# Attention and expert layer on one core: the scores' keys in two halves of the array, and x turned by TensorE in every batch

## Chip, core and metric

The program runs on one core of a Trainium2 chip. The core has five engines that run their own instruction streams in order: TensorE (in the profile PE, its weight loads PEld), VectorE (DVE), ScalarE (ACT), GpSimd (POOL) and SyncE (SP, which here only issues DMAs). They meet at semaphores. The metric is the device time of one execution in microseconds (us), as the median of several runs; less is better.

## What is computed

Attention over 8 batches, 12 heads, 448 tokens and a head size of 64, with root-mean-square norms on q and k, and then a layer of 8 experts that each take the 448 best tokens.

```python
q_n, k_n = rmsnorm(q, g_q), rmsnorm(k, g_k)
scores = np.matmul(q_n, k_n.transpose(0, 1, 3, 2)) / np.sqrt(64)
scores = scores - np.max(scores, axis=-1, keepdims=True)
attn = np.exp(scores)
attn = attn / (np.sum(attn, axis=-1, keepdims=True) + 1e-09)
x = np.matmul(attn, v)                      # (8, 12, 448, 64) -> 3584 tokens of 768
logits = x @ w_gate                         # 3584 x 8: the best 448 tokens for each expert, greedily
out[mask] = np.maximum(x[mask] @ w1[e], 0.0) @ w2[e]        # for each expert e
```

## The kernel before

**Tiling.** The attention works on 24 groups of four heads (three groups a batch); in a group two pairs of heads lie side by side. A head pair has seven units of up to 128 keys: per head three blocks of 128 keys, and one unit (u = 3) with the last 64 keys of both heads. q and k are split into two float16 parts, a high and a low one, that lie above each other in the 128 rows, so a unit's scores are two accumulating passes (`k1` by `q1`, `k2` by `q2`). One score task d makes two units into a tile `psc` of PSUM (ring of 2), and ScalarE makes `e` of it with one exp.

**What TensorE does in the attention**, with its lines in the profile:
- `max_score` (L482, L485): cheaper scores for the row maxima, in the tile `pm` (ring of 1) and one of `psc`; VectorE reduces them (`max_reduce`, L496). The maxima go back as a row into `q2`: ScalarE scales them into `qm`, a DMA turns them (L436, `mt<-qm`), two more put them into `q2` (L443, `q<-mt`). The scores of the group need that row.
- `scores` (L519 for a unit of 128 keys: one matmul fills all 128 columns of the array; L514 for u = 3: two matmuls, each in 64 columns of the array, write the lower and upper 64 partitions of `psc`).
- `av` (L544): e by v, always as two matmuls in 64 columns each. They are float32, and the trace shows two matmuls for each that the program has.
- `gate` (L648 to L656): the router's logits from `xt`, which is x with its features on the partitions.

The array's form, rows by columns in use, stands in the profile's rows: 128\*128 (L519, gate), 128\*64 (L514, L544, L655), 64\*128 and 64\*64 (maxima).

**x.** VectorE divides by the sums, ScalarE makes the high part of x (`x_hi`, L582), VectorE the low one (`x_lo`, L588 and L589), per head pair, into `xb` and `xm`. `x_store` writes them to memory for the experts. `xt` is made from the same tiles: in batches 0 to 6 by four DMA transposes per batch on SP's queue (`x_dma_turn`, L597 and L599); in the last batch by TensorE, per head pair hp, as soon as its x is there (`x_turn`, L623 and L626, into `pm` or `psc`, and `x_turned`, L636 on ScalarE or L638 on VectorE, from PSUM to `xt`).

**Order.** Every task has a number, and a table written out by hand of two characters per task (`ORDER`) gives the order in which all are emitted; an engine takes its own in that order. So the order on each engine is fixed, and only semaphores decide when each starts. The router and the experts follow when the attention is done, and TensorE is the only engine that is nearly always busy there too.

Of the kernel before, what the change touches and what calls it, by code (L numbers as in the profile page):

```python
# [26 lines left out]
F32 = mybir.dt.float32  # L27
F16 = mybir.dt.float16
# [61 lines left out]
class Attention:  # L90
# [500 lines left out]
    def x_dma_turn(self, b, part):  # L591
        nc = self.nc
        if part == 0:
            self.T["xt", b] = self.w.tile([128, 42, 128], F16, name="xt", bufs=1)
        t, xb, xm = self.T["xt", b], self.T["xb", b], self.T["xm", b]
        if part < 3:
            nc.sync.dma_start_transpose(t[:, 12 * part:12 * part + 12], xb[:, part].rearrange("p i c -> p (i c)"))  # L597
        else:
            nc.sync.dma_start_transpose(t[:, 36:], xm.rearrange("p i h d -> p (i h d)"))  # L599

# [11 lines left out]
    def x_turn(self, b, hp):  # L612

        nc = self.nc
        if hp == 0:
            self.T["xt", b] = self.w.tile([128, 42, 128], F16, name="xt", bufs=1)
        t, xb, xm = self.T["xt", b], self.T["xb", b], self.T["xm", b]
        p = self.ps.tile([128, 2, 512], F32, name=("pm", "psc")[hp % 3 > 0], bufs=1 + (hp % 3 > 0))
# [8 lines left out]
        self.T["tp", hp] = p  # L627

    def x_turned(self, b, hp, mid):
        p, t = self.T["tp", hp], self.T["xt", b]  # L630
# [4 lines left out]
        if hp < 4:  # L635
# [56 lines left out]
    def gate_sum(self, b):  # L692
# [21 lines left out]
                 V=2, mx=2, pm=1, psc=2, e=9, po=2, z=2, xb=2, xt=1, lsc=2)  # L714
    GATE = 3

    def plan(self):
# [136 lines left out]
        for pair in range(2 * self.NG):  # L854
# [13 lines left out]
            if hp == 5:  # L868
# [3 lines left out]
                if b < last:  # L872
                    for i in range(4):
                        add(s + P["xst"] + P["xstep"] * i, "S", 1.75 if i < 3 else 1.3, self.x_dma_turn, b, i, after=x, opens=[("xt", b)],
                            make=("xt", b, i), uses=[("xb", b)], move=(1.3, 1.5 if i < 3 else 0.75))
                if b < last:
                    for j in range(4):
                        add(s + P["gate"] + P["gates"] * j, "T", US["gate"], self.gate, b, j,
                            after=[*(("xt", b, i) for i in range(4)), "wg"], make=("pg", b), opens=[("gate", b)] if j == 0 else (),
# [5 lines left out]
                else:  # L885
                    add(s + P["gate"] + 0.2, "D", 0.2, self.gate_copy, b, after=[("pg", b)], make=("logits", b),
                        frees=[("pg", b)])
            if b == last:
                ring = ("pm", "psc")[hp % 3 > 0]
                add(s + P["xturn"], "T", US["xturn"], self.x_turn, b, hp, after=[x[hp], x[hp - hp % 2]],  # L890
                    make=("tp", hp), opens=[("xt", b)] * (hp == 0), holds=[(ring, ("xt", hp))], uses=[("xb", b), ("xt", b)])
                for mid in range(1 + hp % 2):
                    q = "AD"[hp > 3]
                    add(s + P["xtd"] + mid, q, US[f"xtd{q}{mid}"], self.x_turned, b, hp, mid,
                        after=[("tp", hp)], make=("xt", b, hp), uses=[("xt", b)], frees=[("xt", hp)])
# [8 lines left out]
    def plan_first(self, plan, g, a, t):  # L904
# [1021 lines left out]
```

## Time and profile before

| | us |
|---|---|
| median of 3 runs | 953.76 (952.52 to 955.08) |
| the profiled execution | 957.85 |
| its span, from the first instruction to the last | 956.0 |
| TensorE busy (matmuls) | 887.7 |
| VectorE, ScalarE, GpSimd busy | 625.0, 465.4, 400.1 |

The attention takes the first 456 us of the span, the router and the experts the rest. A group of rows below gives an engine's busy time in a stretch, another the waits, others single instructions with their start in us. TensorE's matmuls overlap: of two rows of the timeline the difference of their starts is what the first one costs, not its own length.

### The profile page before, as it was taken

To read this page: it belongs to the slowest core of one execution; us is meant where nothing else is said; L and a number is where in the kernel's file an instruction comes from. 1 tells how busy PE (TensorE), PEld (TensorE's weight loads), DVE (VectorE), ACT (ScalarE), POOL (GpSimd) and SP (SyncE) were. 2 spreads that over 40 slices of the span, in tenths; PEclk is the share of its full clock that TensorE was granted. 3 is DMA by queue.
4 is the path that set the end of the run, shared out by engine and by line. 5 is a ranking of instruction groups with operands and counts; after the bars stand their busy time and mean duration, and the time that the engine had idled before them with its cause. 6 is when DMAs were issued, how large, how long until landed. Compare 5 with 4: busy or idle time off the path is not lost.

```text
span 956.0 us, 25484 instructions
## 1 busy us (share of the span) xinstructions
PE 887.7 (93%) x10674; PEld 542.4 (57%) x10676; DVE 625.0 (65%) x1468; ACT 465.4 (49%) x705; POOL 400.1 (42%) x447
## 2 busy tenths in 40 slices
PE   2878989998999998999699999899999999999996
PEld 1445556665666655668465556456565555655553
DVE  6877877886677776963788777576876757234110
ACT  4866667766778676655044433333333424243110
POOL 7697878788688886720110302011112020120001
PEclk9999999999999999999599999999999999999998
DMA  6456889979899988961374929495967649483001
GB/s 165 106 121 138 172 164 205 187 182 198 191 181 218 179 202 162 181 106 58 97 256 159 274 84 222 143 250 181 217 205 221 201 148 298 150 179 119 25 18 41
DMA packets 271787, 157.84 MB, mean 165 GB/s; under 512 B 197398, under 2 KB 258838, under 8 KB 270648
## 3 DMA queue, kind: packets, MB, share of 16 engines
q1 hardware_dynamic: 247128, 129.33, 58.0%
q0 software_dynamic: 4704, 22.10, 7.7%
q10 hardware_dynamic: 19840, 4.79, 2.4%
q8 instruction: 83, 1.36, 0.6%
q14 instruction: 32, 0.26, 0.1%
HBM read 94.49 MB, written 22.02 MB: 122 GB/s over the span
## 4 chain that ended last, share of the span: by engine, by line
issue 34%; PE 8%; POOL 5%; DVE 2%; DMA 1%; SPq 1%; ACT 0%; POOLq 0%; DVEq 0%
PE ph L1689 6%; POOL rows L1622 2%; POOL out_dram L1725 2%; PE py L1706 1%; DMA stage<-in_moe_w_dram 1%; SPq L1627 1%; PE py L1655 1%; PE rp L1264 0%; DMA rows<-xd,idx 0%; POOL spacer L1724 0%; DVE or L1239 0%; DVE cmp L1249 0%; PE rp L1335 0%; ACT xt L1642 0%; ACT w2h L1605 0%
## 5 line engine op out<-in xcount | busy, mean ns | idle before, releaser
L1689 PE MATMUL ph<-xt,w1h 128*128 128x448 f16 (+2 forms) x804 | 209.7, 344 | 0.3 <-ACT xt L1642 0.3
L544 PEld LDWEIGHTS po<-v,e 128*64 128x64 f32 x5376 | 177.2, 139 | 55.3 <-issue 45.9
L544 PE MATMUL po<-v,e 128*64 128x65 f32 x5376 | 198.4, 226 | 0.9 <-DVE xm L589 0.5
L530 ACT ACTIVATE e<-psc 128x896 f32<-128x896 f32 x168 | 152.0, 916 | 83.1 <-PE psc L519 55.0
L1725 POOL DMA_INDIRECT out_dram<-y,idx x32 | 32.6, 1018 | 292.2 <-ACT y L1708 256.8
L519 PE MATMUL psc<-q,k 128*128 128x448 f16 x576 | 137.3, 360 | 10.4 <-DMA q<-mt 6.4
L1689 PE MATMUL ph<-xt,w1l 128*128 128x448 f16 (+2 forms) x402 | 135.1, 344 | 0.0
L1706 PE MATMUL py<-w2h,hl 128*128 128x384 f16 x384 | 125.0, 326 | 0.0
L1706 PE MATMUL py<-w2h,hh 128*128 128x384 f16 x384 | 125.0, 326 | 0.0
L1706 PE MATMUL py<-w2l,hh 128*128 128x384 f16 x384 | 125.0, 326 | 0.0
L496 DVE TENSOR_REDUCE mx<-pm 128x2 f32<-128x896 f32 x96 | 103.9, 1083 | 27.7 <-PE pm L485 22.2
L1689 PEld LDWEIGHTS <-w1h 128*128 128x128 f16 x804 | 74.0, 97 | 63.8 <-issue 2.1
L1677 ACT ACTIVATE hh<-ph 128x448 f16<-128x448 f32 x64 | 34.8, 544 | 143.7 <-PE ph L1689 142.0
L1706 PEld LDWEIGHTS <-hh 128*128 128x128 f16 x768 | 73.2, 97 | 46.7
L1679 DVE SCALAR_TENSOR_TENSOR hl<-ph,hh 128x448 f16<-128x448 f32 x64 | 39.3, 618 | 73.0 <-ACT hh L1677 72.9
L496 DVE TENSOR_REDUCE mx<-psc 128x2 f32<-128x896 f32 x74 | 78.1, 1058 | 10.8 <-PE psc L485 10.0
L1622 POOL DMA_INDIRECT rows<-xd,idx x32 | 32.2, 1005 | 125.3 <-PE rp L1457 65.8
L1708 ACT ACTIVATE y<-py 128x384 f32<-128x384 f32 x48 | 23.6, 491 | 124.8 <-PE py L1706 98.6
L519 PEld LDWEIGHTS <-k 128*128 128x128 f16 x576 | 46.3, 98 | 52.1 <-issue 15.7
L1609 DVE SCALAR_TENSOR_TENSOR w2l<-stage,w2h 128x768 f16<-128x768 f32 x64 | 60.1, 951 | 14.7 <-ACT w2h L1605 14.4
L1609 DVE SCALAR_TENSOR_TENSOR w1l<-stage,w1h 128x768 f16<-128x768 f32 x64 | 59.3, 950 | 3.3 <-ACT w1h L1605 3.3
L277 DVE TENSOR_REDUCE st<-sq 128x14 f32<-128x910 f32 (+1 forms) x52 | 52.4, 1017 | 11.3 <-ACT sq L265 8.9
(282 smaller groups left out, 1399.7 us busy)
## 6 DMA issues: line engine op xcount, KB each, us to landing
stage<-in_moe_w_dram SPq DMA_DIRECT2D x64, 768.0 KB
vraw<-in_v_dram SPq DMA_DIRECT2D x24, 384.0 KB
xd<-xb SPq DMA_DIRECT2D x8, 1152.0 KB
qkraw<-in_q_dram SPq DMA_DIRECT2D x23, 384.0 KB
qkraw<-in_k_dram SPq DMA_DIRECT2D x23, 384.0 KB
xd<-xm SPq DMA_DIRECT2D x16, 96.0 KB
qkraw<-in_k_dram ACTq DMA_DIRECT2D x46, 32.0 KB
qkraw<-in_q_dram ACTq DMA_DIRECT2D x44, 32.0 KB
```

The costliest lines, as they stand in the source:

```text
L277: self.nc.vector.tensor_reduce(self.stat(g, 0, a)[:, i], self.T["sq", g, i][:, self.of(a)], axis=AX.X, op=OP.add)
L496: self.nc.vector.tensor_reduce(m, p[:, :k, :448], axis=AX.X, op=OP.max)
L519: nc.tensor.matmul(p[:, i, :448], kt[:, a, n:n + 128], qt[:, a, 448 * s:448 * s + 448], start=st, stop=not st)
L530: self.nc.scalar.activation(e, p[:, :, :448], AF.Exp, scale=scale)
L544: nc.tensor.matmul(out, self.T["e", d][:, i, q0:q0 + m], self.v1[g % 2][:, self.slot(a, u, s)], start=u == us[0], stop=u == us[-1])
L1609: self.later(0.93, lambda w=w: self.nc.vector.scalar_tensor_tensor(l[:, w], v[:, w], self.WS, h[:, w], op0=OP.mult, op1=OP.subtract), k, i)
L1622: nc.gpsimd.indirect_dma_start(out=g[:n, c, :], out_offset=None, in_=self.xd, in_offset=bass.IndirectOffsetOnAxis(ap=idx[:n, c:c + 1], axi ...
L1677: nc.scalar.activation(hh, whole, AF.Relu)
L1679: self.later(0.6, lambda: nc.vector.scalar_tensor_tensor(hl, whole, 0.0, hh, op0=OP.max, op1=OP.subtract), k, 3.5, f)
L1689: nc.tensor.matmul(p, a[:, i, c], x[:, b, o], start=j == 0, stop=j == 17)
L1706: nc.tensor.matmul(p, a[:, f, s], b[:, f, o], start=st, stop=sp)
L1725: st = nc.gpsimd.indirect_dma_start(out=self.out, out_offset=bass.IndirectOffsetOnAxis(ap=self.router.idx[k][:n, c:c + 1], axis=0), in_=y[ ...
```

## The change

`scores` makes every unit as it made u = 3: two matmuls, each with 64 keys in 64 columns of the array and the same queries, in the two halves of `psc`'s partitions. `x_dma_turn` is gone; `x_turn` and `x_turned` run in every batch, in batches 0 to 6 always with the tile `pm` and with VectorE. `xt` has two buffers instead of one. The table of the order has a number for each new task.

```diff
-                if u == 3:
-                    for s in range(2):
-                        nc.tensor.matmul(p[64 * s:64 * s + 64, i, :448],
-                                         kt[:, a, 384 + 64 * s:448 + 64 * s],
-                                         qt[:, a, 448 * s:448 * s + 448], start=st, stop=not st)
-                else:
-                    s = u // 4
-                    nc.tensor.matmul(p[:, i, :448], kt[:, a, n:n + 128],
+                for h in range(2):
+                    s = h if u == 3 else u // 4
+                    nc.tensor.matmul(p[64 * h:64 * h + 64, i, :448], kt[:, a, n + 64 * h:n + 64 * h + 64],
                                      qt[:, a, 448 * s:448 * s + 448], start=st, stop=not st)
...
-    def x_dma_turn(self, b, part):
...
-            nc.sync.dma_start_transpose(t[:, 12 * part:12 * part + 12], xb[:, part].rearrange("p i c -> p (i c)"))
...
+    def turn_ring(self, b, hp):
+        return ("pm", "psc")[hp % 3 > 0] if b == self.B - 1 else "pm"
+
+    def turned_queue(self, b, hp):
+        return "A" if b == self.B - 1 and hp < 4 else "D"
...
-        if hp < 4:
+        if self.turned_queue(b, hp) == "A":
             self.nc.scalar.activation(o, p, AF.Copy)
         else:
             self.nc.vector.tensor_copy(o, p)
...
-                 V=2, mx=2, pm=1, psc=2, e=9, po=2, z=2, xb=2, xt=1, lsc=2)
+                 V=2, mx=2, pm=1, psc=2, e=9, po=2, z=2, xb=2, xt=2, lsc=2)
...
-        "4H3XDv36HzN5DwN23u4ISC3v3ZDyDxN63wNADz3a4KH+3xD+D-3zN8E03CH-I03+4hSDSE37NB4jSF384LI1NC3yI24J4kSGE14i410ESHN7"
+        "4H3XDv36HzN5DwN23u4ISC3v3ZDyDxN63wNADz3a4KH+3xD+D-3zN8E03CH-I03+4hSFSG37NB4jSH384LI1SDSENC3yI24J4kSIE14i410E"
```

All other tasks keep their places among each other on every engine; the new ones stand between them, and SP's queue loses 28 DMA transposes. TensorE, one score unit between two stretches of `av` (`k_902` and `q_1025` are one group's keys and queries, `k_1_126` and `q_0_128` the tiles `k2` and `q2`), before:

```order
631 L544 MATMUL po<-v_1_137,e 64x65 x16
632 L519 LDWEIGHTS k_902
633 L519 MATMUL psc<-q_1025,k_902 128x448
634 L519 LDWEIGHTS k_1_126
635 L519 MATMUL psc<-q_0_128,k_1_126 128x448
```

and after (the `av` ahead is L539 now; the numbers of the buffers differ):

```order
1048 L539 MATMUL po<-v_0_136,e 64x65 x8
1049 L514 LDWEIGHTS k_959
1050 L514 MATMUL psc<-q_1097,k_959 64x448
1051 L514 LDWEIGHTS k_959
1052 L514 MATMUL psc<-q_1097,k_959 64x448
1053 L514 LDWEIGHTS k_1_126
1054 L514 MATMUL psc<-q_0_128,k_1_126 64x448
1055 L514 LDWEIGHTS k_1_126
1056 L514 MATMUL psc<-q_0_128,k_1_126 64x448
```

Each matmul of 128 output partitions has become two of 64. SP's queue around the first batch's x (`mt` is the turned row of maxima on its way to `q2`), before:

```order
55 L436 DMA_TRANSPOSE mt<-qm_131 128x1x128
56 L597 DMA_TRANSPOSE xt<-xb 128x12x128
57 L443 DMA q_1_129<-mt 1x7x128 x2
58 L386 DMA_TRANSPOSE k_1716<-ks_1510 128x14x128
59 L597 DMA_TRANSPOSE xt<-xb 128x12x128
60 L386 DMA_TRANSPOSE q_1775<-qs_1699 128x14x128
```

and after:

```order
54 L436 DMA_TRANSPOSE mt<-qm_131 128x1x128
55 L443 DMA q_1_129<-mt 1x7x128 x2
56 L386 DMA_TRANSPOSE k_1900<-ks_1655 128x14x128
57 L386 DMA_TRANSPOSE q_1967<-qs_1882 128x14x128
```

The turns of x no longer stand between the maxima's row and the transposes of k and q. TensorE behind a new turn of x, after (there is no L609 or L612 at this place before; L485 follows the scores directly):

```order
3874 L609 MATMUL pm<-ident,xb 128x128
3875 L612 LDWEIGHTS xm
3876 L612 MATMUL pm<-ident,xm 128x128
3877 L612 LDWEIGHTS xm
3878 L612 MATMUL pm<-ident,xm 128x128
3879 L485 LDWEIGHTS q_5807
3880 L485 MATMUL pm<-k_1_126,q_5807 128x448
```

The maxima behind it use the same tile `pm`, so they follow VectorE's copies out of it. VectorE in batch 6 (L1124 to L1164 are a piece of the router that the attention takes in), after:

```order
541 L1134 TENSOR_SCALAR key<-keyi 128x21
542 L1164 TENSOR_TENSOR cmp<-key,hit_80 128x672
543 L630 COPY xt<-pm 128x6x128
544 L630 COPY xt<-pm 128x2x128
545 L630 COPY xt<-pm 128x6x128
546 L496 TENSOR_REDUCE mx<-pm 128x2
```

Two turns' copies stand behind the router's piece and ahead of the next reduction.

## Rows read from the trace of the kernel before

**Rows 1.** Busy time of each engine in stretches of the attention: bounds in us, their length, then PE, PEld, DVE, ACT and POOL busy with their counts, TensorE's granted clock as a share of 2.4 GHz, the mean share of the DMA engines, GB/s. The last line sums seven stretches from 100 to 440 us.

```profile
60.00:100.00 40.00, 33.69 (x540) 21.13 (x539) 32.26 (x48) 26.27 (x42) 33.13 (x33) 0.96 0.68 134
...
150.00:200.00 50.00, 49.00 (x868) 31.77 (x868) 39.10 (x65) 36.88 (x61) 40.20 (x39) 1.00 1.00 180
200.00:250.00 50.00, 46.08 (x794) 29.40 (x793) 37.37 (x63) 32.04 (x54) 41.35 (x40) 0.97 0.96 205
...
400.00:440.00 40.00, 40.00 (x768) 27.00 (x766) 21.57 (x44) 23.31 (x38) 7.90 (x8) 1.00 0.67 130
sum 340.00, PE 323.21 PEld 211.73 DVE 251.87 ACT 230.43 POOL 250.21; mean PE 46.17 PEld 30.25 DVE 35.98 ACT 32.92 POOL 35.74
```

**Rows 2.** What TensorE waited for from 100 to 440 us: the waiting line, what ended the wait; us in total, times, longest.

```profile
PE psc L519 <- DMA q<-mt: 4.9, 5, 1.7
PE pm L485 <- DVE mx L496: 3.6, 3, 3.2
PE psc L519 <- ACT e L530: 2.6, 6, 0.7
PE psc L485 <- ACT e L530: 1.9, 2, 1.2
PE pm L485 <- DMA q<-qs: 1.3, 1, 1.3
...
PE po L648 <- DMA xt<-xb: 0.6, 1, 0.6
```

**Rows 3.** TensorE in order of time at three places: start, length, line, operation, output and inputs, array form, shape, count.

```profile
397.90 1.62 PE L544 MATMUL po<-v,e 128*64 128x65 f32 x48
399.45 0.93 PE L519 MATMUL psc<-q,k 128*128 128x448 f16 x4
400.31 0.69 PE L544 MATMUL po<-v,e 128*64 128x65 f32 x16
400.93 0.36 PE L485 MATMUL pm<-k,q 64*128 64x448 f16 x2
...
414.72 0.55 PE L519 MATMUL psc<-q,k 128*128 128x448 f16 x2
415.20 0.57 PE L514 MATMUL psc<-q,k 128*64 128x448 f16 x4
415.60 0.63 PE L544 MATMUL po<-v,e 128*64 128x65 f32 x16
416.17 0.36 PE L485 MATMUL pm<-k,q 64*128 64x448 f16 x2
...
429.66 3.49 PE L544 MATMUL po<-v,e 128*64 128x65 f32 x112
432.97 0.17 PE L655 MATMUL po<-wg,xt 128*64 128x16 f16 x1
```

**Rows 4.** TensorE in the experts, first and last of 21 rows without a gap, each two matmuls in 64 columns of the array.

```profile
943.75 0.33 PE L1715 MATMUL py<-w2h,hh 128*64 128x384 f16 x2
...
947.00 0.33 PE L1715 MATMUL py<-w2h,hl 128*64 128x384 f16 x2
```

**Rows 5.** The last batch's turns of x in order of time: TensorE (L623, L626) and the row behind it, VectorE's copies out of PSUM (L638), and the weight load (PEld) that follows the first copy.

```profile
440.21 0.50 PE L623 MATMUL pm<-ident,xb 128*128 128x128 f16 x6
440.55 0.92 PE L519 MATMUL psc<-q,k 128*128 128x448 f16 x4
...
446.57 0.50 PE L623 MATMUL pm<-ident,xb 128*128 128x128 f16 x6
...
447.01 0.50 PE L623 MATMUL psc<-ident,xb 128*128 128x128 f16 x6
...
451.55 0.50 PE L623 MATMUL psc<-ident,xb 128*128 128x128 f16 x6
452.08 0.56 DVE L638 COPY xt<-psc 128x768 f16<-128x768 f16 x1
452.69 0.10 PEld L668 LDWEIGHTS <-xt 128*128 128x128 f16 x1 [0.17 <-DVE xt L638]
...
454.07 0.76 DVE L638 COPY xt<-psc 128x256 f16<-128x256 f16 x2 [0.53 <-PE psc L626]
```

**Rows 6.** SP's DMA transposes of x: line, operation, count, shortest, median and longest ns on SP's queue, first and last start; and two rows of SP's queue in order of time.

```profile
L597 SPq DMA_TRANSPOSE xt<-xb x21: 1386/2016/3305, 111.0 to 420.2; - x21
...
L599 SPq DMA_TRANSPOSE xt<-xm x7: 1211/1317/2097, 133.0 to 421.9; - x7
...
228.12 1.87 SPq L597 DMA_TRANSPOSE xt<-xb  x1
...
231.84 1.60 SPq L443 DMA_DIRECT2D q<-mt  x2
```

**Rows 7.** VectorE's reductions of `pm` among the page's costliest groups (busy us, mean ns of one, idle before and its releaser); then, from the timeline, VectorE's first and last instruction of the router's piece, and TensorE where it ends.

```profile
L496 DVE TENSOR_REDUCE mx<-pm 128x2 f32<-128x896 f32 x96 | 103.9, 1083 | 27.7 <-PE pm L485 22.2
...
390.90 0.33 DVE L1135 TENSOR_REDUCE best<-logits 128x21 f32<-128x168 f32 x1
...
396.55 0.86 DVE L1175 TENSOR_TENSOR cmp<-key,hit 128x672 bf16<-128x672 f32 x1
...
396.39 1.10 PE L544 MATMUL po<-v,e 128*64 128x65 f32 x32
397.42 0.36 PE L485 MATMUL pm<-k,q 64*128 64x448 f16 x2
```

More of the change, by code (lines that the diff above doesn't have):

```diff
@@ L589, in x_lo @@
         tt(om[:, 1], m, om[:, 0], op=OP.subtract)
-    def x_dma_turn(self, b, part):
[L592 to L596, printed above, removed]
-            nc.sync.dma_start_transpose(t[:, 12 * part:12 * part + 12], xb[:, part].rearrange("p i c -> p (i c)"))
-        else:
-            nc.sync.dma_start_transpose(t[:, 36:], xm.rearrange("p i h d -> p (i h d)"))
     def x_store(self, b, part):
@@ L615, in x_turn @@
         if hp == 0:
-            self.T["xt", b] = self.w.tile([128, 42, 128], F16, name="xt", bufs=1)
+            self.T["xt", b] = self.w.tile([128, 42, 128], F16, name="xt", bufs=self.RINGS["xt"])
         t, xb, xm = self.T["xt", b], self.T["xb", b], self.T["xm", b]
-        p = self.ps.tile([128, 2, 512], F32, name=("pm", "psc")[hp % 3 > 0], bufs=1 + (hp % 3 > 0))
+        ring = self.turn_ring(b, hp)
+        p = self.ps.tile([128, 2, 512], F32, name=ring, bufs=self.RINGS[ring])
         p = [p[:, i].bitcast(F16).rearrange("p (n c) -> p n c", c=128) for i in range(2)]
@@ L872, in plan @@
                 if b < last:
[L873 to L876, printed above, removed]
                     for j in range(4):
                         add(s + P["gate"] + P["gates"] * j, "T", US["gate"], self.gate, b, j,
-                            after=[*(("xt", b, i) for i in range(4)), "wg"], make=("pg", b), opens=[("gate", b)] if j == 0 else (),
+                            after=[*(("xt", b, i) for i in range(6)), "wg"], make=("pg", b), opens=[("gate", b)] if j == 0 else (),
                             uses=[("xt", b), ("gate", b)], holds=[("po", ("pg", b))] if j == 0 else (), modes=[int(j == 3)] * 2)
@@ L887, in plan @@
                         frees=[("pg", b)])
-            if b == last:
[L889 to L895, printed above, removed]
+            ring, q = self.turn_ring(b, hp), self.turned_queue(b, hp)
+            add(s + P["xturn"], "T", US["xturn"], self.x_turn, b, hp, after=[x[hp], x[hp - hp % 2]],
+                make=("tp", b, hp), opens=[("xt", b)] * (hp == 0), holds=[(ring, ("xt", b, hp))], uses=[("xb", b), ("xt", b)])
+            for mid in range(1 + hp % 2):
+                add(s + P["xtd"] + mid, q, US[f"xtd{q}{mid}"], self.x_turned, b, hp, mid,
+                    after=[("tp", b, hp)], make=("xt", b, hp), uses=[("xt", b)], frees=[("xt", b, hp)])
+            if b == last:
                 add(s + P["glast"], "T", 0.25 + 0.34 * (hp % 2), self.gate_last, b, hp,
@@ new lines @@
+        "ITNYEO5h4zNc47SlIU5KEPSmNd5L4-IVNe5MSnEQ0r5j4+NaERNf5lESIW5N5kNk5m50IXETNZ5OEV5QIY51EUNb48IZNg68S+Ia5nS-4ZNh"
+        "Ib5oEW6BIc6C5P4eT0IeEXT1IdNjT2Nl5R4a694bIfSxIg4gNiSySzEY5pT55qT6NmIhEZNn4AT7No6AEa4cT3NqT8Ii5r5ST40I0J0KT9Eb"
+        "5sIj5UNsEc6DNpEd5TEeNtEf4fNvEg5tTANx5V6ENrIk5vNyTBTC0LTD6G6F5uImIlTENwTF5W4d6HEhIoIn57EiTGNz6d6IIpIqTH52TINu"
+        "53Ir5wIs54TJTKTLTMSrItStSqIuTNSoSuIv0MTOEjSsEk6e6JN+Sv6fIwEl5x55TPO06KIxO3TQTREm6i6gSwO25y56EoO46h5zEnO56LOA"
+        "6jEp5+O9Er6M6OIyEqI+595XIz6P6kO8I-O1766lEs5-J06NEt58N-J2J1TSTT6mO75Y77J35ZJ4TU6nOBTV796oO6J5SpJ6TZ7B5cTaTW6p"
@@ new lines @@
+        "Eu6QTbOC6q5aEvJ7ODTcOH7ATXOITd5dJ8TYEw5eOE6R6SJ9ExOG0N0OEz78JA6r6TEyJCJBOF5b6sE+JD7bTqTrOJE-6tJE7gF0TnOM6U7C"
+        "ToTpTsF1OLF26u7EOKTtJG7F61JF62ONOOJH7D60JI6vTuOPJJ7eTvJK7G7c6wTwF363JLOQ0PF47dOVTxF5JM7HOTTyJNTz7IF67fORF77J"
+        "OUF8JO6yT+7KOST-JPF9OWFB7h7L84OX6xFA7MJQ85OaU3U47NU5FC6VOc7jJSJR65ObU6FDU0TgOdJTJUU766867kOZ6z6W64OYU1U2U87i"
+        "JVJW6XU9UAJYUBJXUC87ThUDTi89JaUEJZTjOe88676YFE7OOj0Q0RFFJbTk7POh7QFG7l7m8AFHOkFJ8C7nOf6aTl6cFI7oJc7ROiTmJdOg"
+        "7pFK6b6+Ol0SFM6ZJe7q7rFLJg7SJfUIFNUJJhOp8ZFOOn8dUKJi8b8DUFOmUL6-Oq8aUGUHUMJj70Jk8BUNJm73JlTeOo8E7tTfUOFP7sOs"
@@ new lines @@
+        "JnFQ71Ot8fFROr7u8e8cJoUPUQURFSJp7vOvFTOy8FUSFUOu758G7TFVUTOx8IFX7wJq8gOw8H8hOzUgUhJrO+0T0U8iJs8J748K7xFWP0Jt"
+        "Ui92JuUjO-JvJw94FYJxP3FZJyUk7UFa72P28jJzFb8LP17V93FcP4FdUnUoPA8kFe8M8lP9FfJ+8m95977WP7UpJ-Fg8NP6UqK0987YUrP8"
+        "Fi8n968O7XP5K18oUvK27aUwFh8PUdK4K3UxK5UeUfUlUmFjUXUZUaK67yUyUYK70V0WUzK8997ZPB8QK9PGFk8rUsKAUW9A9XPD8s81PFUb"
+        "7z0XUtUuU+9B827+PHKBPCU-UcPI9C8pUUFlKC9D9bFm8q9cPEFn9YPLKDV0PK7-V1V29ZFoKEFpPOV39E8tFqPJ9FKFPNV4Fr9aKGFt9G9I"
+        "8uPPFsKHKI9H83PS80FuKJPM8v9dPQ8RKKV89fV9VAKMKLFvA0PVKN9gV5KOA2VBPR8SA1V6V7VC9K8TFwPTFxKP9LA3PWA48WFyPUVDKQVE"
@@ L990 @@
+        "Y0Y1HcMVReY4MWHdY5CuRgRfDIMXMYDJY6MaMZYADHYBYCXvMbXxMcYDXwDLYEMeDKRiMdRkRjMfXtRlXuRoRnXsRmXyMgXzX+YJMiMhRpMj"
+        "RrRqYKYLRsMkYMRtMlRuRvMmYRYNY7MnMoRwYSMpYTRyRxYUMqY8YVRzMrS0R+R-MsYaYbYcYWMtYFYdS1YGS3S2YHYeS5S7S6S4YOYiYjY9"
+        "YkYPYfYIYlYgYXYhYmYQYYYpYrYZYtYoYsYnYuYq"
     )
```

56 lines of the change are left out of this document (20 added, 36 removed).

## The prediction

> **What bounds the kernel now.** I read the busy times by stretch first [rows 1]. From 100 to 440 us TensorE's matmuls fill 323 of 340 us, VectorE 252, GpSimd 250 and ScalarE 230. From 400 to 440 us TensorE is busy without a break. So in the attention the time is TensorE's, made of its own work and of what it waits for. The waits came next [rows 2]: on DMAs 4.9 + 1.3 + 0.6 = 6.8 us, on VectorE's reductions 3.6, on ScalarE's exp 2.6 + 1.9 = 4.5. From 150 to 200 us the DMA engines are busy all the time and TensorE still is for 49 of 50 us: busy DMA engines cost nothing there. From 60 to 100 us TensorE is busy for 33.7 of 40 us; less work on it may be lost there. Then I read the timeline of TensorE [rows 3], because busy time hides what a change of the array's form costs: the difference of two starts shows it. The change leaves the router and the experts alone, so I look for everything in the attention.
>
> **Part 1, the scores in two halves.** Prices, from differences of starts [rows 3]. Forty-eight matmuls of av take 1.55 us and sixteen take 0.62: 0.029 for one, and 0.155 for the stretch. The 112 that are followed by L655, which has the same form 128\*64, take 3.31 = 112 x 0.029 + 0.05. So of the 0.155 some 0.105 goes with the change of form behind the stretch and 0.05 with the one ahead; av behind L514 agrees, sixteen in 0.57. Four full score matmuls take 0.86 and two 0.48: 0.19 each, and 0.10 for the change of form behind them. Two pairs of L514 take 0.40: 0.19 a pair, and 0.02 for the change ahead. So av to full scores costs 0.105, full scores to av 0.10 + 0.05 = 0.15, full scores to L514 0.10 + 0.02 = 0.12.
>
> A pair in two halves costs what one full matmul did. The experts' pairs of 384 columns start (947.00 - 943.75) / 20 = 0.1625 apart [rows 4], which is 0.1896 for 448 columns. So the work itself stays the same, and the changes of form go: in the order of before av is followed by full scores 110 times, full scores by av 70 times and by L514 48 times: 110 x 0.105 + 70 x 0.15 + 48 x 0.12 = 11.6 + 10.5 + 5.8 = 27.8 us. The order of after has 187 places between scores and av, all of one form. Where this stall goes, ScalarE's exp is late next: TensorE already waits for it at eight places [rows 2], with a shorter score task by up to 0.1 us more each. That, and the first 100 us, where TensorE waits for others anyway, may take back some of it: I put 0.4 us for both, and 2 into the range.
>
> The Trainium skill speaks against this part: in "TensorEngine Tiling (Array Packing)", section Restrictions and Gotchas, columns in tiles exclude Fast Weight Load. By that rule weight loads would come to stand ahead of the pairs, a score unit would be longer than before, and the time would be that of the third rival below. The trace has such pairs without a loss [rows 4], so I go by the trace.
>
> **Part 2, x turned on TensorE.** New are 42 turns, 21 of six matmuls and 21 of eight. Six start 0.34 us before the next work, eight 0.44 [rows 5]: 21 x 0.34 + 21 x 0.44 = 16.4 us. A turn has the form 128\*128 and mostly stands between works of the form 128\*64. By the order: 25 times av ahead (0.105), 20 times scores (0.10), 21 times av behind (0.15), 19 times scores (0.12) = 2.6 + 2.0 + 3.2 + 2.3 = 10.1, less 0.5 for those that the last batch had already: 9.6. Together 26.0 us. So part 1 gives 27.8 / 8 = 3.5 us a batch and part 2 takes 26.0 / 7 = 3.7 in the seven batches that get it: **TensorE's work stays the same to 2 us** (-27.8 + 26.0 = -1.8), and what is left lies in the last batch, where TensorE is busy without a break [rows 1].
>
> The Trainium skill gives a far higher price for a turn: "TensorE: Matmul & The Clock Gate", Part 4, has some 275 ns for one 128x128 turn in a kernel. By that the 294 turns would cost 81 us instead of 16.4. In this trace they start 56 ns apart [rows 5], so I take the trace.
>
> **Part 3, the copies out of PSUM.** A turn in `pm` is copied by VectorE: 0.56 us for six blocks, 0.76 for eight [rows 5], so 21 x 0.56 + 21 x 0.76 = 27.7 us more on VectorE, which goes from 252 to some 276 of 340 us (three of the turns lie before 100 us). It keeps idle time, but `pm` has one buffer. From the start of a turn to the next use of `pm` go 2.08 - 1.55 = 0.53 us until the copy begins, 0.56 for it and 0.05 until TensorE follows: 1.14 us; for eight blocks some 1.4. Behind 3 of the 42 turns the maxima that need `pm` follow directly (as in the third place of the order above): 0.8 us of wait each for six blocks, 1.0 for eight. Behind nine more one stretch of scores or av stands between, 0.6 to 0.9 us, which covers the copy if VectorE takes it up at once; it is busy for three quarters of the time, so I take 0.2 each. One place is worse: two turns' copies stand behind the router's piece, which holds VectorE from 390.9 to 397.4 [rows 7]; the maxima at 397.42 then have the rest of one copy, a turn and a copy ahead, some 2 us (one of the three directly followed is this one). Sum: 2 x 0.9 + 2 + 9 x 0.2 = 5.6. The copies also push other rows of VectorE back by up to 0.4 us more than the turn itself delays TensorE; where a reduction is already late (3.6 us, [rows 2]) that adds up, and I take 1 us. So **6.6 us of new waits**; with VectorE free at every copy 2.6 + 1, with a reduction of 1.08 us [rows 7] ahead of it at all twelve places 2.6 + 2 + 13.
>
> **Part 4, DMAs taken away.** SP loses 21 issues of 2.0 us and 7 of 1.3 [rows 6], 51 us of a queue that runs in order, and the DMA engines lose the traffic. What stands behind these issues is the row of maxima on its way to `q2`: at 231.84 its DMAs start behind a turn of x at 228.12 [rows 6]. The waits that this can end are the 6.8 us on DMAs and the slower clock behind them (0.97 of 2.4 GHz in the stretch 200 to 250 us [rows 1], so 3% of 50 us, 1.5 us; before it stand waits on `q<-mt`): 8.3 at most, and nothing at least, since fewer transfers make none later. Not every such wait has a turn of x ahead. I take **5.5 us**.
>
> **Sum.** -1.8 + 0.4 + 6.6 - 5.5 = -0.3 us. The profiled execution is 957.85 us, its span 956.0 with 1.85 around it, and 4.1 above the median 953.76; the sum says 957.5 for such an execution and, moved to the median, 953.5. I forecast **953.5**, no change that can be told: a difference under 0.3% (2.9 us) is about what a measurement of this kernel can tell from none.
>
> **Rivals.**
> - The DMAs' relief arrives in full and `pm` doesn't bind: -1.8 - 8.3 + 2.6 = -7.5, so 946. For it: a turn can begin only when `pm`'s last reduction is over, so VectorE is often free for its copy, and the DMA engines were full. Against it: the exp and the reductions, on which TensorE waits for as long, get nothing.
> - Slower by the ring: VectorE takes up a copy one reduction late. It decides from the point at which a copy comes while a reduction runs and the next maxima stand within 1.1 us behind the turn, which is so at twelve places: 12 x 1.08 + 2.6 + 2 = 17.6 instead of 6.6, so +11 against the forecast, 964.5. Against it: VectorE is idle for a quarter of the time, and the reduction that it may be in is one of `psc` or of squares, since that of `pm` is over.
> - The pairs lose their weight loads' cover. Priced by the 0.02 that a first pair pays, on 576 former full matmuls: +11.5, so 965. Against it [rows 4]. It is what the skill's page on tiling would lead to.
> - Turns that don't overlap with what follows: 0.50 us each instead of 0.34 [rows 5], 42 x 0.16 = +6.7, so 960. The skill's 275 ns is this case at its worst (+64 us, by that page).
>
> **Chances.** Forecast 0.50 (own range 950 to 957: 0.38 within 0.3%, 0.09 faster, 0.03 slower), relief 0.26, ring 0.15, pairs 0.05, turns 0.04. So faster 0.09 + 0.26 = 0.35, same 0.38, slower 0.27. The range of 8 in 10 reaches to 945 for the relief with 1.5 us around it, and to 962, which takes in the milder half of the ring and leaves its upper half and the pairs out.
>
> **What would show it.** Score stretches between av should take 0.76 us for two units (0.86 before), and sixteen matmuls of av between scores 0.47 (0.62): if not, part 1 is wrong. Six turns should take 0.34 to the next start and show no wait of their own. Waits of TensorE on `q<-mt` and `q<-qs` should fall from 6.2 us to under 2, and new ones on VectorE's `xt` copies should come to 4 to 8 us, with one of some 2 us where the router's piece ends. The forecast is wrong if TensorE's waits as a whole, some 15 us in [rows 2], move by more than 3 us.

## The result and the profile after

The kernel after takes 961.13 us (median of 20 runs, 954.16 to 966.07), the kernel before beside it 954.3 (20 runs, 946.46 to 964.74): a ratio of 1.0076, 95% interval 1.0052 to 1.0100. It is slower by 7.2 us by the ratio (6.8 by the medians), where no change was forecast (953.5). Medians are of all runs; ratios leave out the executions that fell into a slower state of the chip, so the two can differ by some us. The profiled execution has a span of 959.4 us, against 956.0.

Busy times by stretch, the columns as in [rows 1]; the last line again sums 100 to 440 us:

```profile
60.00:100.00 40.00, 34.59 (x610) 24.20 (x609) 32.99 (x52) 25.85 (x43) 33.42 (x33) 0.96 0.63 137
...
200.00:250.00 50.00, 47.24 (x953) 34.64 (x950) 40.95 (x75) 33.63 (x57) 42.78 (x41) 1.00 0.75 186
...
400.00:440.00 40.00, 39.92 (x829) 30.78 (x831) 25.29 (x49) 22.17 (x36) 8.20 (x8) 0.96 0.38 101
sum 340.00, PE 322.45 PEld 239.82 DVE 274.74 ACT 229.06 POOL 249.85; mean PE 46.06 PEld 34.26 DVE 39.25 ACT 32.72 POOL 35.69
```

VectorE's 23 us more are the copies, and the DMA engines are no longer full (0.96 to 0.75 from 200 to 250 us). TensorE is as busy as before. What it waited for from 100 to 440 us, the answer to [rows 2]:

```profile
PE psc L514 <- ACT e L525: 4.2, 6, 1.2
PE pm L485 <- DVE mx L496: 3.7, 4, 2.5
PE pm L609 <- DVE mx L496: 2.2, 2, 1.8
PE pm L609 <- DVE xt L630: 1.0, 1, 1.0
PE psc L485 <- DVE mx L496: 1.0, 2, 0.6
...
PE pm L482 <- DVE xt L630: 0.9, 2, 0.7
...
PE pm L485 <- DVE xt L630: 0.7, 1, 0.7
...
PE psc L514 <- DMA q<-mt: 0.4, 1, 0.4
```

The waits on DMAs are gone but for 0.4 us (6.8 before), and as much wait on VectorE has come in their place: 11.2 us in all against 4.7, of which 2.6 are on the copies `xt` and most of the rest on reductions. TensorE in order of time, the answer to [rows 3, 5]:

```profile
161.89 0.51 PE L609 MATMUL pm<-ident,xb 128*128 128x128 f16 x6
162.33 0.69 PE L539 MATMUL po<-v,e 128*64 128x65 f32 x16
...
393.79 0.92 PE L514 MATMUL psc<-q,k 128*64 128x448 f16 x8
394.55 1.57 PE L539 MATMUL po<-v,e 128*64 128x65 f32 x48
395.95 0.92 PE L514 MATMUL psc<-q,k 128*64 128x448 f16 x8
...
406.65 0.64 PE L539 MATMUL po<-v,e 128*64 128x65 f32 x16
407.12 0.93 PE L514 MATMUL psc<-q,k 128*64 128x448 f16 x8
```

By the starts, two units of scores take 0.76 us, sixteen matmuls of av 0.47, forty-eight 1.40, and six turns with the change of form behind them 0.44: each price is the one forecast. The last view is the router's piece, VectorE's last row of it and what TensorE does there, the answer to [rows 7]:

```profile
396.71 1.10 PE L539 MATMUL po<-v,e 128*64 128x65 f32 x32
...
397.17 0.86 DVE L1164 TENSOR_TENSOR cmp<-key,hit 128x672 bf16<-128x672 f32 x1
398.04 0.76 DVE L630 COPY xt<-pm 128x768 f16<-128x768 f16 x2
...
398.85 0.49 PE L609 MATMUL pm<-ident,xb 128*128 128x128 f16 x6 [1.04 <-DVE xt L630]
...
400.08 0.36 PE L485 MATMUL pm<-k,q 64*128 64x448 f16 x2 [0.74 <-DVE xt L630]
...
400.60 2.87 PE L539 MATMUL po<-v,e 128*64 128x65 f32 x48
403.25 1.25 PE L514 MATMUL psc<-q,k 128*64 128x448 f16 x8
```

The two waits of 1.04 and 0.74 us are the 2 us that were forecast there. But the 48 matmuls of av behind them take 2.65 us instead of 1.40: the granted clock is 0.50 of 2.4 GHz there, 1.2 GHz (columns as in [rows 1]).

```profile
402.00:403.60 1.60, 1.60 (x30) 1.44 (x28) 0.68 (x2) 0.00 (x0) 0.00 (x0) 0.50 0.02 6
```

From the first av matmul to the last the attention takes 412.74 us before and 415.36 after, TensorE busy and the rest (columns as in [rows 1]). Before, and after:

```profile
38.08:450.82 412.74, 386.78 (x6864) 253.46 (x6865) 302.50 (x501) 279.67 (x455) 301.61 (x289) 0.98 0.84 168
```

```profile
38.56:453.92 415.36, 388.69 (x7725) 288.36 (x7725) 326.36 (x564) 278.87 (x455) 301.18 (x289) 0.98 0.66 144
```

TensorE is idle for 26.0 us before and 26.7 after. This line, and idle = length less busy, is the measure for what follows. It differs between executions of one kernel: a second one of before, and two of after in which the experts were changed (further down), have

```profile
38.24:449.55 411.31, 385.55 (x6864) 252.66 (x6865) 300.43 (x501) 278.64 (x455) 301.52 (x289) 0.99 0.82 168
```

```profile
38.95:449.35 410.40, 385.46 (x7724) 285.89 (x7725) 325.77 (x564) 278.88 (x455) 301.49 (x289) 0.99 0.66 146
```

```profile
39.55:449.15 409.60, 385.50 (x7725) 285.82 (x7725) 326.23 (x564) 278.71 (x455) 301.29 (x289) 0.99 0.66 146
```

### The profile page after: what moved, and what is told of

The parts are those of the page before. It is cut to its first block, busy times and chain, and to the rows that moved or that the text cites. A ratio compares the mean times of both kernels' runs of the same rounds, so it can differ in the third digit from the quotient of the medians.

```text
span 959.4 us, 27248 instructions
## 1 busy us (share of the span) xinstructions
PE 888.0 (93%) x11546; PEld 576.8 (60%) x11546; DVE 649.0 (68%) x1531; ACT 464.3 (48%) x705; POOL 399.1 (42%) x447
## 4 chain that ended last, share of the span: by engine, by line
issue 34%; PE 10%; POOL 5%; DVE 2%; POOLq 0%; DVEq 0%
PE ph L1678 6%; POOL rows L1611 2%; PE py L1695 2%; POOL out_dram L1714 2%; PE py L1704 0%; PE rp L1253 0%; POOL spacer L1713 0%; DVE or L1228 0%; PE rp L1324 0%; DVE cmp L1238 0%; DVE w1l L1598 0%; DVE xt L1633 0%; PE py L1626 0%; POOLq L1910 0%; DVE or L1480 0%
## 5 line engine op out<-in xcount | busy, mean ns | idle before, releaser
L539 PEld LDWEIGHTS po<-v,e 128*64 128x64 f32 x5376 | 184.8, 140 | 37.6 <-issue 21.0
L539 PE MATMUL po<-v,e 128*64 128x65 f32 x5376 | 198.3, 226 | 1.2 <-DVE xm L584 0.8
L514 PE MATMUL psc<-q,k 128*64 128x448 f16 x1344 | 157.2, 359 | 6.2 <-ACT e L525 4.5
L514 PEld LDWEIGHTS <-k 128*64 128x64 f16 x1344 | 72.4, 111 | 42.1 <-issue 13.6
L1611 POOL DMA_INDIRECT rows<-xd,idx x32 | 32.1, 1004 | 124.0 <-PE rp L1446 65.2
L1594 ACT ACTIVATE w1h<-stage 128x1536 f16<-128x1536 f32 x32 | 47.3, 1477 | 22.1 <-DMA stage<-in_moe_w_dram 22.0
```

The costliest lines, as they stand in the source:

```text
L514: nc.tensor.matmul(p[64 * h:64 * h + 64, i, :448], kt[:, a, n + 64 * h:n + 64 * h + 64], qt[:, a, 448 * s:448 * s + 448], start=st, stop=n ...
L539: nc.tensor.matmul(out, self.T["e", d][:, i, q0:q0 + m], self.v1[g % 2][:, self.slot(a, u, s)], start=u == us[0], stop=u == us[-1])
L1594: self.nc.scalar.activation(h, v, AF.Copy, scale=self.WS)
L1611: nc.gpsimd.indirect_dma_start(out=g[:n, c, :], out_offset=None, in_=self.xd, in_offset=bass.IndirectOffsetOnAxis(ap=idx[:n, c:c + 1], axi ...
```

## The experiments

All ratios are to the kernel before, runs of the same chip; 0.001 is 0.95 us. Theory A says that the prices of the four parts were right and one place, the router's piece, went wrong. Theory B says that TensorE's time was counted wrongly: work that is taken from it comes back as waits. Where an expectation names a theory A or B and says what it means, it is one of its own.

### The scores alone

```diff
 # the kernel before, with the new scores()
+                for h in range(2):
+                    nc.tensor.matmul(p[64 * h:64 * h + 64, i, :448], kt[:, a, n + 64 * h:n + 64 * h + 64], ...
```

Expected: 

> The kernel before with the scores in two halves; x is turned by DMA as before. By the prediction's prices the changes of form go, 27.8 us, less what ScalarE's exp, the maxima's row and the full DMA queue take back once TensorE is faster: a ratio of 0.971 if nothing takes any back, 0.980 to 0.985 if a third to a half is lost to them. If halves cost TensorE something that the two traces do not show, the ratio is 0.995 or more.

Measured: 945.65 us, 0.9927 (0.9901 to 0.9953). The attention and its waits:

```profile
38.27:443.19 404.92, 367.60 (x7431) 273.64 (x7431) 299.51 (x501) 278.36 (x455) 301.07 (x289) 0.97 0.85 171
```

```profile
PE psc L514 <- DMA q<-mt: 8.6, 5, 4.4
PE psc L514 <- ACT e L525: 6.5, 8, 2.9
PE pm L485 <- DVE mx L496: 3.7, 3, 3.2
PE pm L485 <- DMA q<-qs: 2.6, 2, 1.5
```

TensorE is busy 19.2 us less and idle 11.4 more (37.3). Three quarters of the 27.4 us that part 1 gives are not in the time, more than the third to a half that was expected. This fits theory B.

### The turns alone

```diff
 # the kernel after, with the old scores()
+                    nc.tensor.matmul(p[:, i, :448], kt[:, a, n:n + 128], ...
```

Expected: 

> The kernel after with full scores of 128 keys, as before; the turns of x stay on TensorE. By the prediction's prices the scores' changes of form come back, some 27 us less about 5 for turns that then stand beside work of their own form: 22 us above the kernel after, 29 above the kernel before, a ratio of 1.031 to the latter. If ScalarE, VectorE or the maxima's row sets the pace in the kernel after, a slower TensorE hides some of it: 1.015 to 1.025.

Measured: 962.47 us, 1.0098 (1.0068 to 1.0129), less than either expectation.

```profile
38.13:458.43 420.30, 402.75 (x7159) 270.53 (x7159) 324.44 (x564) 280.15 (x455) 301.34 (x289) 0.99 0.67 142
```

TensorE is busy 16.0 us more than before and idle 8.4 less (17.6). By the ratios (1.0098 and 1.0076, whose intervals overlap) the halves bring the kernel after only 2 us in the company of the turns, though its TensorE is busy 14.1 us less: 9.1 of them are idle time again in these two traces. But this run's attention is longer than all three of the kernel after, by 5 to 11 us (420.30 against 415.36, 410.40 and 409.60), and its experts are 4.7 us shorter (458.2 from their first matmul to their last, against 462.9). So the ratio of whole runs hides part of what the halves do in the attention.

### The router's piece moved

```diff
 # the kernel after; the table of the order, batch 6 (hp 1 and 2 are the pairs behind the router's piece)
-early, x_turn(6,1), ..., x_turned(6,1,0), x_turned(6,1,1), x_turn(6,2), x_turned(6,2,0), max_scores(156), ..., max_reduce(156)
+x_turn(6,1), x_turned(6,1,0), x_turned(6,1,1), early, ..., max_scores(156), ..., max_reduce(156), x_turn(6,2), x_turned(6,2,0)
```

Expected: 

> The kernel after, with the router's piece on VectorE moved behind the first turn's copies, and the second turn with its copy moved behind the next maxima of the same ring. Theory A, that the time was lost at this one place (1.0 + 0.7 us of waits at 398 to 400 us, and 3.4 us at half the clock behind them, worth 1.6): 3.0 to 3.5 us less than the kernel after, a ratio of 1.0035 to 1.0045 to the kernel before. Theory B, that the new turns cost time at many places and this is only the one that this execution shows: at most 1 us less, 1.006 to 1.008.

Measured: 959.97 us, 1.0067 (1.0037 to 1.0098). That lies where this expectation's theory B has it, but the interval takes in theory A too. Its attention took 410.90 us, 4.5 less than in the first trace of the kernel after but not less than in the other two, and its experts 3.2 us more than in the first: 466.1 against 462.9. The experts come below.

### The DMA turns left out

```diff
 # the kernel before
+        if b == 0 and part == 0:
+            self.fixed = self.w.tile([128, 48, 128], F16, name="xt", bufs=1)
+        self.T["xt", b] = self.fixed[:, b:b + 42]
+        if b > 0:
+            return
...
```

Expected: 

> The kernel before without the DMA turns of x in batches 1 to 6: the router's logits of these batches are made from shifted views of the first batch's turned x, so the choice of tokens is another one, with the same amount of work everywhere. This is the DMAs' relief alone, without the turns on TensorE. The prediction took 5.5 us (6/7 of it here, 4.7: a ratio of 0.995); in full it would be 8.3 (7.1 here, 0.9925). Theory A, that the waits on DMAs in the profiled execution, which was 3.5 us above the median, were more than the usual ones: 1 to 2.5 us, 0.9975 to 0.999. If no wait of the usual execution has such a transfer ahead: 1.000.

Measured: 948.12 us, 0.9945 (0.9914 to 0.9977): 5.2 us, where the prediction has 4.7 for these six batches. Its price for the DMAs' relief agrees; the interval, 2.2 to 8.2 us, takes in the full relief (7.1) as well, and little of the doubt in the expectation (1 to 2.5).

```profile
38.12:445.20 407.08, 386.12 (x6864) 253.20 (x6865) 300.86 (x501) 279.10 (x455) 301.63 (x289) 0.98 0.70 150
```

### Both gains without a price

The last edit together with the new `scores`.

Expected: 

> The kernel before with the scores in two halves and without the DMA turns of x in batches 1 to 6: the router's logits of these batches are made from shifted views of the first batch's turned x, so the choice of tokens is another one, with the same amount of work. It is the two gains without any turn on TensorE or copy. With the halves alone TensorE's work fell by 22 us and the time by 7, and its waits on the maxima's row (10.9 us) and on q (2.6) were DMA waits. If the DMAs keep the halves' gain back, both go with the turns: 928 to 933 us, a ratio of 0.974 to 0.979. If the two gains only add up, 0.9927 and 0.9945: 0.987. If ScalarE and VectorE pace TensorE by now: 0.990 or more.

Measured: 933.07 us, 0.9769 (0.9728 to 0.9809): 22 us. The halves alone bring 7, the DMA turns left out 5, both together 22. In the attention alone, against the mean of four traces of before (411.64 us, all four are listed below), it is 6.7, 4.6 and 19.5. So the DMA turns kept the halves' gain back: the waits on the row of maxima, `q<-mt`, fall from 8.6 us to 1.8, while those on `q<-qs` stay (2.6 and 2.7).

```profile
38.52:430.64 392.12, 364.68 (x7430) 272.39 (x7431) 300.28 (x501) 277.82 (x455) 301.17 (x289) 0.98 0.73 156
```

```profile
PE psc L514 <- ACT e L525: 7.6, 11, 2.3
PE pm L485 <- DVE mx L496: 3.6, 3, 3.2
PE pm L485 <- DMA q<-qs: 2.7, 1, 2.7
PE psc L514 <- DMA q<-mt: 1.8, 2, 1.4
```

Against the run before this one TensorE is busy 21.4 us less, not 27.8, and idle 6.5 more. Most of that is on DMAs once again: from the first av matmul to the last the waits on them go from 1.3 us to 6.6, and those on ScalarE's exp from 8.9 to 11.1.

### The copies: left out, and on ScalarE

```diff
 # the kernel after; first run of the two
+        if 0 < b < self.B - 1:
+            return        # in x_turned; xt of these batches is a view of the first batch's
 # second run
-        return "A" if b == self.B - 1 and hp < 4 else "D"
+        return "A" if b < self.B - 1 or hp < 4 else "D"
```

Expected without them: 

> The kernel after without the copies of turned x out of PSUM in batches 1 to 6; TensorE still makes the turns, and the router's logits of these batches come from shifted views of the first batch's turned x, so the choice of tokens is another one. VectorE has 23.8 us less to do, and the ring of the maxima is free as soon as a turn is over. If the copies are what keeps the halves' gain back in the kernel after, 6 to 10 us less than it: a ratio to the kernel before of 0.997 to 1.001. If only the waits on the copies go, 2.6 us, and at the router's piece 3.3: 1.001 to 1.004. If ScalarE's exp and the maxima's reductions are late without them too: 1.005 to 1.008.

Expected on ScalarE: 

> The kernel after with all copies of turned x out of PSUM on ScalarE instead of VectorE. If VectorE's load is what holds the kernel after up (7 us of TensorE's waits there are on reductions, 3 on the copies themselves), it is 3 to 6 us faster than the kernel after: a ratio to the kernel before of 1.001 to 1.005. If ScalarE's exp is as late as VectorE's reductions (TensorE waits 7 us for it in the kernel after), the waits only move: 1.006 to 1.014.

Measured: without the copies 952.12 us, 0.9968 (0.9942 to 0.9995); on ScalarE 971.47, 1.0165 (1.0114 to 1.0216). So by whole runs the 36 turns' copies cost the kernel after 9 us by the medians, 10 by the ratios. On ScalarE the time is above both expectations; it is the worse place, and the same ring then waits for it.

```profile
PE pm L609 <- ACT xt L628: 5.8, 7, 2.0
PE pm L485 <- ACT xt L628: 4.6, 6, 1.2
PE pm L482 <- ACT xt L628: 3.8, 5, 1.3
```

The attention without the copies, in the slowest of its twelve executions (957.07 us):

```profile
38.85:449.02 410.17, 385.27 (x7724) 285.72 (x7725) 306.02 (x511) 278.93 (x455) 301.90 (x289) 0.99 0.67 146
```

With the copies it was 415.36, 410.40 and 409.60 us. So the traces show between 5 us and nothing for the copies in the attention, and the 9 to 10 us of the whole runs are not found there. These runs don't separate the ring from VectorE's load either.

### The kernel before again

Expected: 

> The kernel before once more, for a second execution with a profile: the ratio is 1.000. If the waits on DMAs of the first profile (6.8 us from 100 to 440 us) are usual, this profile shows 5 to 8 us of them again; if they were much by chance, under 4.

Measured: 954.02 us, 0.9974 (0.9944 to 1.0005). Its profile has 5.8 us of waits on `q<-mt` and 2.6 on `q<-qs`: usual waits, not chance (8.4 us together, just above the 5 to 8 expected). Its attention took 411.31 us.

### One expert alone

```diff
-        for k in range(8):
+        for k in range(1):        # in the experts; the lists for k = 1 to 7 are left out too
```

Expected before: 

> The kernel before with the first expert alone: the attention and the router's first choice are whole, the other seven experts are left out. In the experts TensorE waits up to 6 us for VectorE around 550 to 605 us in some executions, whatever the change; here that part is gone, and the time is that of the attention. From the profiled executions: attention to 450.5, router 33.5, first expert some 60 to 80 us, end 9.

Expected after: 

> The kernel after with the first expert alone, the other seven left out. If the whole of the 7 us of the medians lies in the attention: 6 to 8 us above the kernel before with one expert. If the profiled executions tell the usual attention, 453.9 against 450.8 and 449.6: 3 to 4.5 us above, and the rest is the experts'.

Expected with the router's piece moved: 

> The kernel after with the router's piece moved (as in the third experiment) and the first expert alone, the other seven left out. Theory A, that the one place at the router's piece costs the kernel after 3.3 us (1.8 of waits and 1.6 of half clock): 2.8 to 4 us below the kernel after with one expert. Theory B, that this place is only where one execution shows what is lost elsewhere in another: less than 1 us below.

Measured: 545.26 (ratio 0.5708, 0.5681 to 0.5735), 547.85 (0.5741, 0.5714 to 0.5767) and 545.54 us (0.5718, 0.5692 to 0.5744). So the attention and the first expert account for 2.6 us of the 7 by the medians, 3.2 by the ratios, below what was expected for either case; the move of the router's piece gives back 2.3 of them, between its two theories. The intervals are wider than these differences. In the profile of the second run the router's place has the same two waits as in the kernel after (for the second the profile names a DMA that ended last):

```profile
395.84 0.49 PE L609 MATMUL pm<-ident,xb 128*128 128x128 f16 x6 [1.05 <-DVE xt L630]
397.07 0.37 PE L485 MATMUL pm<-k,q 64*128 64x448 f16 x2 [0.74 <-DMA vraw<-in_v_dram]
...
397.56 1.62 PE L539 MATMUL po<-v,e 128*64 128x65 f32 x48
399.01 0.93 PE L514 MATMUL psc<-q,k 128*64 128x448 f16 x8
```

The 48 matmuls of av take 1.45 us: the clock did not fall this time. In the third run neither wait is there.

### The experts' waits taken away

One place where the experts differ between executions is a pair of DMA transposes of the third expert's tokens. SP's queue in the kernel before and with the scores alone, and the wait of TensorE behind the first:

```profile
583.79 11.19 SPq L1627 DMA_TRANSPOSE xt<-rows  x2
...
603.92 0.17 PE L1349 MATMUL rp<-cs,sums 128*128 128x8 f16 x1 [2.65 <-DVE cs L1345]
```

```profile
575.33 6.13 SPq L1622 DMA_TRANSPOSE xt<-rows  x2
```

The pair holds the queue for some 6 us or some 12, and behind it stands a load of weights, ScalarE's and VectorE's split of them, and the router's step on which TensorE waits. With 6 us the experts take 457.6 us (scores alone), with 12 they take 462.5 (before), 462.9 (after) and 466.1 (router's piece moved). The seven other traces that have all experts and these transposes go the same way: 457.6 to 458.2 us where the pair takes 5.7 to 5.9 (turns alone, both gains, SP's queue in another order), 462.1 to 464.1 where it takes 11.3 to 12.0 (before again, DMA turns left out, copies left out, copies on ScalarE). So a ratio of whole runs can hold 4 to 8 us of the experts where two kernels differ in this. The pair is not the only place: four of the seven slower ones also wait 1.6 to 2.6 us some 63 us behind the experts' first matmul.

```diff
-    HERE = {0: (0, 1, 2, 3), 1: (2, 3)}
+    HERE = {0: (0, 1, 2, 3), 1: (2, 3), 2: (0, 1, 2, 3)}
```

Expected before: 

> The kernel before, with the third expert's tokens turned on TensorE instead of by DMA transposes, as the first expert's are already; these transposes held SP's queue for up to 12 us around 585 us and with it a load of weights that TensorE then waited for. The turns cost TensorE some 3 us; the waits behind them (2 to 6 us, and half the clock behind them) should be gone: 948 to 953 us, with less scatter than the 946 to 965 of the kernel before.

Expected after: 

> The kernel after with the same change in the experts as the run before this one. If the 7 us between the medians are the attention's 2.6 (as with one expert alone) and otherwise how often the experts lose these waits: 2 to 4 us above the other of this pair. If the kernel after is slower by 7 us in its attention: 6 to 8 above.

Expected with the scores alone: 

> The scores in two halves, x turned by DMA, and the third expert's tokens turned on TensorE. With the halves alone no profiled execution lost time at this place, so only the turns' own cost is left: 946 to 949 us. If it is nevertheless lost in some, 942 to 945.

Expected with the router's piece moved: 

> The kernel after with the router's piece moved (as in the third experiment) and the third expert's tokens turned on TensorE. With one expert alone the move gave back 2.3 us of the 2.6; so here 2 to 3.5 below the kernel after of this group, and within 1 of the kernel before of this group. If the place at the router's piece is not what costs the kernel after its time: within 1 of the kernel after of this group.

Measured: 955.3 (0.9998, 0.9968 to 1.0028), 957.08 (1.0047, 1.0017 to 1.0078), 948.14 (0.9935, 0.9909 to 0.9961) and 956.45 us (1.0020, 0.9996 to 1.0044). The first was expected at 948 to 953, and the scatter did not go: it still ranges from 949.41 to 965.87, so these transposes are not its only cause. Between the first two stand 1.8 us by the medians and 4.7 by the ratios; the move of the router's piece gives back 0.6 or 2.6.

### SP's queue in another order

```diff
 # the scores alone; the table of the order: eight of the 28 x_dma_turn behind row_max of the group, one gate behind another
-tr_max(17), x_dma_turn(4,3), ..., row_max(17)
+tr_max(17), ..., row_max(17), x_dma_turn(4,2), x_dma_turn(4,3)
```

Expected: 

> The scores in two halves, x turned by DMA, and of the 28 DMA turns eight that stand on SP's queue between the turn of the maxima's row and its way to q2, or shortly ahead of it, behind it instead. With the halves alone TensorE waited 10.9 us for that row, 4.4 of it at 333 us with two such turns ahead. If the queue's order is what makes the row late: 3 to 8 us below the halves alone, 938 to 943. If the DMA engines are simply full, whatever the order: 945 as before.

Measured: 950.46 us, 0.9960 (0.9932 to 0.9988): 5 us worse than the scores alone by the medians and 3 by the ratios, whose intervals overlap. It is no gain, where 3 to 8 us or nothing had been expected.

```profile
PE psc L514 <- ACT e L525: 8.9, 14, 2.2
PE psc L514 <- DMA q<-mt: 4.6, 5, 1.7
PE pm L485 <- DMA q<-qs: 4.0, 3, 3.2
...
PE po L643 <- DMA xt<-xb: 3.2, 2, 2.3
```

The row of maxima is earlier as meant (4.6 us of waits instead of 8.6), but now the gates wait for `xt` and the maxima for `q`: the same DMA work, late at another place. Of the versions that compute the whole, the scores alone, 945.65 us, are the fastest; they beat both kernels.

## Why the prediction was wrong

The terms, for the batches that the runs cover. The whole runs are differences between the ratios of neighbouring runs, times 954.3, so that they add up; the attention is its length in the traces, with the mean of four for before and of three for after.

| | predicted, us | whole runs, us | attention, us |
|---|---|---|---|
| part 1 and part 4 together | -27.4 - 4.7 = -32.1 | -22.0 | -19.5 |
| part 2, turns without copies, on top | +26.0 | +19.0 | +18.1 |
| part 3, the copies of six batches, on top | 6.6 x 6/7 = +5.7 | +10.3 | +1.6 (-0.6 to +5.2) |
| sum | -0.4 | +7.3 | +0.2 |

- **The first step that failed is in part 1: "I put 0.4 us for both".** The prices of a start to the next start were right, but their sum was taken as time. With the DMA turns left out the halves bring 16.8 us by the ratios and 15.0 in the attention, not 27.4. TensorE's busy time fell by 21.4 us, not 27.8, and idle time grew by 6.5, more of it in waits on DMAs than on the exp that the prediction had named as late next. Where the rest went, the starts show. Take every stretch of scores and of av at the shortest length that the traces have for as many matmuls between the same neighbours: full scores need 320.8 us so, halves 295.1. That is 25.7 less, so the prices hold to some 2 us. In fact these stretches took 341.3 us without the DMA turns and 326.8 with the halves too, 14.5 less: 7 more are idle, and 4 more lie in stretches that ran longer than their shortest without an idle row.
- **Part 2** was too dear as time by the same error with the other sign: work given to TensorE partly fills waits. By the shortest lengths, of all its work in the attention, the turns need 26.5 us, where 26.0 were forecast; from the run with both gains to the one without copies TensorE is busy 20.6 us more and idle 2.5 less, and the attention is 18.1 longer. That the errors of parts 1 and 2 take each other back to 3 us in the whole runs is luck, not a right sum.
- **Part 3** stays open. In the first trace of after the waits on VectorE from 100 to 440 us grew by 6.5 us, as forecast in sum (6.6), but only 2.6 us of waits are on the copies, where 4 to 8 were to come. The whole runs give the copies 9 to 10 us, the attention between nothing and 5. The forecast place, the router's piece, showed 1.8 us in each of three traces (the kernel after, with one expert, with the third expert's tokens turned by TensorE), against 2 forecast; in the first of them half the clock followed for 3.4 us, some 1.7 us more, for which there was no term. (VectorE's "some 276" would be 278 by the part's own prices; it was 274.7.)
- **Part 4** agrees: 5.2 us for six batches, in a wide interval.
- **The rivals.** Pairs that lose their weight loads' cover, and turns that don't overlap, fall by the rows of the kernel after: 0.76 us for two units, 0.44 for six turns with 0.10 of it the change of form. The relief had its DMA waits end, from 6.8 us to 0.4, but not its other condition: as much wait came back on VectorE. The ring's time, 964.5, is 3.4 us above the measured one, but its mechanism, a copy one reduction late at twelve places for 17.6 us, is not in the trace, which has 2.6 us of waits on copies and 6.5 more on VectorE in all.
- **The second step that failed is "The change leaves the router and the experts alone, so I look for everything in the attention".** With one expert alone 2.6 to 3.2 us of the 7.2 are left, with the third expert's tokens turned by TensorE 1.8 to 4.7. So between 2.5 and 5.4 us of the difference would lie in how much the experts wait, and the whole runs' term of the copies may hold part of them. The four traces of before with the whole attention unchanged have 412.74, 411.31, 412.11 and 410.41 us for it, the three of after 415.36, 410.40 and 409.60: no difference in the mean. They don't settle it, since three of the four executions of before were 3.3 to 4.3 us slower than the median of their runs, and those of after as fast as theirs or up to 2.6 faster; the intervals of the pairs are too wide too. Whether the change causes the experts' part or the executions differ by chance stays open, and with it the cause of most of the 7 us.
- **The signs.** The 0.76 and the 0.47 came as written, the six turns' 0.34 with the 0.10 of the change of form, and the waits on `q<-mt` and `q<-qs` fell under 2 us. But the turns do wait, 2.2 us on reductions and 1.0 on a copy (L609), where no wait of their own was to come. The last test, that the forecast is wrong if TensorE's waits move by more than 3 us in total, was a bad one: before and after they come to some 16.5 us from 100 to 440 us, and the medians differ by 7.

## What to carry to other kernels

An engine that is busy for 95% of a stretch in an ordered schedule is not a bound whose work can be added and subtracted as time: here of 21.4 us taken from it 6.5 came back as idle time with the DMA turns left out, and of 19.2 us 11.4 with them in. Price a saving by who is late next at every place, and look for two gains that hold each other back, as 7 and 5 us here that together were 22. When one kernel's runs scatter by 2%, cut the program at the stage that is changed and time that, often enough, before crediting the stage with the difference.

## What was not expected of the hardware

- The same wait does not always cost the clock: 1.04 + 0.74 us at the router's piece were followed by 3.4 us at 0.50 of 2.4 GHz in one execution and by full clock in two others (1.05 + 0.74 and 1.03 + 0.74).
- The same two DMA transposes of 128 rows held the queue for 6.13 us in one execution and 11.19 in another, of two kernels with the same experts' code; why is open.
